# Batch 0's q and k in quarters, masks of the first four pairs added by TensorE, batch 1's loads from another queue: one change at the start of a fused attention and MLP kernel

## The chip, the cores and the metric

The kernel runs on one core of a Trainium2 chip. Its time is the device time in microseconds (us) of one execution; several executions are taken and their median is given. One more execution is recorded by the hardware profiler, and every duration below is from that one. The engines are named as in the profile: PE (matrix multiplications, with PEld for its weight loads), DVE (vector), ACT (activations), POOL (GpSimd), SP (it only issues transfers here).

## What is computed

Sliding-window attention (each position sees 32 positions to either side) over 8 batches, 8 heads, 576 positions of 64 values, followed by an MLP with an ELU-like activation over all 4608 tokens:

```
mask = |i - j| <= 32
x    = softmax(where(mask, q k^T / 8, -1e9)) v          # heads side by side: 4608 x 512
h    = x @ w_in                                         # 512 -> 2048
out  = where(h > 0, h, exp(min(h, 0)) - 1) @ w_out      # 2048 -> 512
```

Inputs and output are f32; inside, the kernel multiplies in bf16.

## The kernel before, in words

**Attention.** A block is 64 queries of one batch, with the 128 keys around them; 9 blocks a batch, 72 in all. Two blocks make a pair (128 tokens), numbered 0 to 35; pair 4 holds the last block of batch 0 and the first of batch 1. The steps of the start, by their names in the plan:

- **L** (`load_qk`, L214): half of the heads of q or k of a batch, one DMA of 576 KB, into a staging tile `stg` of 96 partitions by 4 heads by 6 positions of 64 values (so 1536 contiguous bytes a piece in memory); there are four such buffers. For batch 0 q is issued from ACT and k from SP, for all other batches both from ACT.
- **C** (`cast`, L222): f32 to bf16 in SBUF. Batch 0: q on DVE, k on ACT (L232, L230). Later batches: POOL (L232).
- **T** (L234): six transposes by PE (96 x 128 each) of two heads, into PSUM. For batch 0 four PSUM buffers are used in turn (`psT` and three of `psH`), later one.
- **E** (L246): the copy from PSUM to `qT` or `kT`, by ACT, or by DVE for k of batch 0 (L255, L257). T and E come eight times a batch.
- **QK** (L288): 16 or 24 small matmuls for the scores of a pair, into `psS`, of which there is one buffer, so QK(i+1) waits for SM(i). It needs all eight E of its batch.
- **SM** (L307): exp over the pair, 128 x 1024, by ACT, into `pu`. No maximum is subtracted.
- **MK** (L312): two multiplications on DVE by 0/1 masks, from `pu` into `pm`.
- **AV** (L324): two groups of eight matmuls with v, which has a column of ones for the softmax's sum; **RN** (L342) divides by it on DVE; **X/XE** (L352, L364, L370) transposes the result by PE and copies it by ACT (by DMA from pair 8 on).

v comes straight as bf16 by POOL's DMAs (**LV**, L265), and DVE copies parts of it into the other half of the partitions for odd blocks of batches 0 and 1 (**SV**, L282, L284). The weights come by POOL's DMAs too (**WI** L466, **WO** L471), in an order with LV that is written out by hand (`RING`, L488). DMAs of POOL wait for the eighth one before them.

**MLP.** Pairs are gathered in tiles (2, 2, then 4 eight times). **H** (L381) makes 128 of the 2048 columns for a tile: 4 matmuls, in three PSUM buffers. EX (exp, ACT, L389), FF (ACT L399 or DVE L401) and GG (DVE, L407 or L410) make the activation; **Y** (L424) multiplies by w_out, and the result is copied out and stored from SP.

**The order.** Each engine works its instructions strictly in the order in which the program has them. That order comes from `Plan` (L21): a list scheduler on the host, run once when the program is built. Each step has an engine, an assumed duration, a rank and steps that it depends on, and in the model the plan takes the ready step of the least rank. Dependences and durations in the plan only make the order; on the chip an instruction waits for data and for buffers to come free, not for the plan. For example (L507) the loads of batch 1 stand behind SM(2):

```
                if b == 1:
                    deps.append(("SM", L1AT))
                if b == 2:
                    deps.append(("LV", 1, 8))
                if b:
                    deps.append(("C", b - 1, nm, half))
                P.op(("L", b, nm, half), "ACT" if b or nm == "q" else "SP", 0.45,
```

Ahead of the plan, POOL builds the masks (L682 to L706) and DVE clears borders (L708 to L715).

Of the kernel before, what the change touches and what calls it, by code (L numbers as in the profile page):

```python
# [8 lines left out]
FP32 = mybir.dt.float32  # L9
BF16 = mybir.dt.bfloat16  # L10
AX = mybir.ActivationFunctionType
# [139 lines left out]
def kernel(  # L151
# [17 lines left out]
    QB = 64  # L169
    NQB = S // QB  # L170
    HP = H // 2
    PR = 96
    TPP = S // PR
    KW = S + 2 * WIN
    NPAIR = N_TOK // 128
    NFO = D_FF // 128
# [19 lines left out]

    ident = const.tile([128, 128], BF16)
    masks = const.tile([128, 4, QB], BF16)
    w_in_sb = const.tile([128, NDO, D_FF], BF16)
    w_out_sb = const.tile([128, NFO, DM], BF16)  # L200
    NKB = 2
# [9 lines left out]
            for b in range(B) for nm in "qk" for hp in range(HP)}  # L211


    def load_qk(b, nm, half, eng):  # L214
        src = {"q": q, "k": k}[nm]
        t = stg.tile([PR, HP, TPP * D], FP32, name="stg", tag="stg")
        eng.dma_start(
            out=t, in_=src[b, half * HP:(half + 1) * HP].rearrange(
                "h (p t) d -> p h (t d)", t=TPP))
        live[nm, b, half] = t  # L220

    def cast(b, nm, half, eng):  # L222
        if (nm, b) not in live:
            live[nm, b] = bfp.tile([PR, TPP, H, D], BF16, name="bf", tag="bf")
        t = live[nm, b]
        src = live.pop((nm, b, half)).rearrange("p h (t d) -> p h t d", t=TPP)
        dst = t[:, :, half * HP:(half + 1) * HP, :].rearrange(
            "p t h d -> p h t d")
        if eng is nc.scalar:
            nc.scalar.copy(dst, src)  # L230
        else:
            eng.tensor_copy(dst, src)  # L232

    def T(b, nm, hp):  # L234
        src = live[nm, b]
        n = 2 * hp + (nm == "k")
        if b == 0 and n % 4:
            pt = psH_p.tile([128, TPP, PR], BF16, name="psH", tag="psH")
        else:
            pt = psT_p.tile([128, TPP, PR], BF16, name="psT", tag="psT")  # L240
        for j in range(TPP):
            nc.tensor.transpose(pt[:, j, :], src[:, j, 2 * hp:2 * hp + 2, :],  # L242
                                ident[0:PR, 0:PR])
        live["T", b, nm, hp] = pt

    def E(b, nm, hp):  # L246
        pt = live.pop(("T", b, nm, hp))
        if nm == "k":
            dst = kT[b % NKB][:, hp, WIN:WIN + S]
        else:  # L250
            dst = qT[b % NKB][:, hp, :]
        dst = dst.rearrange("c (p t) -> c p t", t=TPP)
        src = pt.rearrange("c t p -> c p t")
        if EVAC[b, nm, hp] == "ACT":
            nc.scalar.copy(dst, src)  # L255
        else:
            nc.vector.tensor_copy(dst, src)  # L257
# [9 lines left out]
    def swapped(b, qb):  # L267
        return b < 2 and qb % 2 == 1
# [16 lines left out]
                            vt[QB:128, w0 - 1:w1 - 1:2])  # L285


    def QK(i):  # L288
        psS = psS_p.tile([128, 2, 2, HP, QB], FP32, name="psS", tag="psS")
        for s in range(2):  # L290
            b, qb = divmod(2 * i + s, NQB)
            for h in range(H):
                hp, base = h // 2, 64 * (h % 2)
                rhs = qT[b % NKB][base:base + 64, hp, qb * QB:qb * QB + QB]
                lo = qb * QB
                if swapped(b, qb):
                    parts = ((0, QB, lo + QB), (QB, 128, lo))
                else:
                    parts = ((0, 128, lo),)
                for p0, p1, c in parts:  # L300
                    nc.tensor.matmul(  # L301
                        psS[p0:p1, h % 2, s, hp, :],
                        lhsT=kT[b % NKB][base:base + 64, hp, c:c + p1 - p0],
                        rhs=rhs, start=True, stop=True)
        live["S", i] = psS

    def SM(i):  # L307
        pu = pup.tile([128, 2, 2, HP, QB], BF16, name="pu", tag="pu")
        nc.scalar.activation(pu, live.pop(("S", i)), AX.Exp, scale=SCALE)  # L309
        live["U", i] = pu  # L310

    def MK(i):  # L312
        pu = live.pop(("U", i))
        p = pm[i % NPB]
        for s in range(2):
            b, qb = divmod(2 * i + s, NQB)
            m = masks[:, 1 if qb == 0 else 2 if qb == NQB - 1 else
                      3 if swapped(b, qb) else 0, :]
            mb = _bap(m, [m.ap[0], [0, 2], [0, HP], m.ap[1]])
            dst = p[:, :, s * 2 * QB:s * 2 * QB + QB].rearrange(  # L320
                "p (a two) c -> p two a c", two=2)
            nc.vector.tensor_mul(dst, pu[:, :, s], mb)  # L322
# [131 lines left out]
        p0 += n  # L454
    NT = len(tiles)
    NC0 = 4
    NPX = 8

    P = Plan({"SP": 0.8, "ACT": 0.8, "POOL": 5.2, "DVE": 6.0})
# [18 lines left out]
    def prank(i):  # L478
        return PER * tiles[where[i][0]][0] + PER * (i - tiles[where[i][0]][0]) - LEAD - 16

    casts0 = {("q", 0): "DVE", ("k", 0): "ACT", ("q", 1): "DVE",
              ("k", 1): "ACT"}
    engs = {"DVE": nc.vector, "ACT": nc.scalar, "POOL": nc.gpsimd}
    cdur = {"DVE": 1.05, "ACT": 1.5, "POOL": 1.5}
    SVOF = {}


    RING = ([("LV", 0, 0), ("LV", 0, 2), ("LV", 0, 4), ("WI", 0),  # L488
# [10 lines left out]
    for b in range(B):  # L499
# [1 line left out]
        r0 = need - 60  # L501
        t0 = where[b * NQB // 2][0]
        early = [("H", max(t0 - 2, 0), 2 if b == 2 else 8)] if b > 1 else []
        for half in range(2):
            for nm in ("q", "k"):
                deps = list(early)
                if b == 1:  # L507
                    deps.append(("SM", L1AT))
                if b == 2:
                    deps.append(("LV", 1, 8))  # L510
                if b:
                    deps.append(("C", b - 1, nm, half))
                P.op(("L", b, nm, half), "ACT" if b or nm == "q" else "SP", 0.45,
                     r0 + half, deps,
                     lambda b=b, nm=nm, half=half: load_qk(
                         b, nm, half,
                         nc.scalar if b or nm == "q" else nc.sync),
                     dma=1.85, wt=0.085, solo=0.75)
                eng = casts0[nm, half] if b == 0 else "POOL"
                deps = [("L", b, nm, half)]  # L520
                if b >= 2:
                    deps += [("T", b - 2, nm, hp) for hp in range(HP)]
                P.op(("C", b, nm, half), eng, cdur[eng], need - 30 + half, deps,
                     lambda b=b, nm=nm, half=half, eng=eng:
                     cast(b, nm, half, engs[eng]))
        deps = list(early)
        if b > 1:
            deps += [("WO", c) for c in range(NWC)]
        if b == 0:
            deps.append(("C", 0, "q", 0))  # L530
        if b >= NVB:
            last = ((b - NVB + 1) * NQB - 1) // 2
            deps += [("AV", last, 0), ("AV", last, 1)]
# [22 lines left out]
        for hp in range(HP):  # L556
            for nm in ("q", "k"):
                n = hp * 2 + (nm == "k")
                deps = [("C", b, nm, hp // 2)]
                m = n - (4 if b == 0 else 1)  # L560
                if m >= 0:
                    deps.append(("E", b, "qk"[m % 2], m // 2))
                elif b:
                    deps.append(("E", b - 1, "k", HP - 1))
                P.op(("T", b, nm, hp), "PE", 0.3, need - 36 + 4 * n, deps,
                     lambda b=b, nm=nm, hp=hp: T(b, nm, hp))
                deps = [("T", b, nm, hp)]
                if b >= NKB:
                    last = ((b - NKB + 1) * NQB - 1) // 2
                    deps.append(("QK", last))  # L570
                P.op(("E", b, nm, hp), EVAC[b, nm, hp], 0.7, need - 36 + 4 * n, deps,
                     lambda b=b, nm=nm, hp=hp: E(b, nm, hp))

    for c in range(NWC):
        P.op(("WI", c), "POOL", 0.85, RING.index(("WI", c)) - 999, [],
             lambda c=c: WI(c), dma=2.55, wt=0.1, soft=ring(("WI", c)))
        P.op(("WO", c), "POOL", 0.85, RING.index(("WO", c)) - 999,
             [("C", 0, "k", 1)] if c == 0 else [],
             lambda c=c: WO(c), dma=2.55, wt=0.1, soft=ring(("WO", c)))

    for i in range(NPAIR):
# [3 lines left out]
                for hp in range(HP)]  # L585
        if i:
            deps.append(("SM", i - 1))
        P.op(("QK", i), "PE", 0.5, r, deps, lambda i=i: QK(i))
        deps = [("QK", i)]
        if i >= 2:  # L590
            deps.append(("MK", i - 2))
        P.op(("SM", i), "ACT", 1.05, r, deps, lambda i=i: SM(i))
        deps = [("SM", i)]
        if i >= 2:
            deps += [("AV", i - 2, 0), ("AV", i - 2, 1)]
        P.op(("MK", i), "DVE", 1.0, r, deps, lambda i=i: MK(i))
        t, c = where[i]
        for g in range(2):
            deps = [("MK", i)]
            for x in (2 * i, 2 * i + 1):  # L600
                b, qb = divmod(x, NQB)
                if qb % 2 == 0:
# [76 lines left out]
    with tc.manual_schedule():  # L679
# [11 lines left out]
        for lo, key in ((0, QB), (QB, 0)):  # L691
# [12 lines left out]
            fill=0.0, base=(128 - WIN) - 1, pattern=[[0, QB]],  # L704
            channel_multiplier=-1)
        nc.gpsimd.tensor_copy(masks, mf)  # L706
        for t in vw:
            nc.vector.memset(t[0:WIN, 0, :, 0:D], 0.0)  # L708
            nc.vector.memset(t[128 - WIN:128, NQB - 1, :, 0:D], 0.0)
            nc.vector.memset(t[:, 0:NQB:2, :, D:VW], 1.0)  # L710
# [36 lines left out]
```

## Time and profile before

| | us |
|---|---|
| median of 11 runs | 343.91 (342.13 to 346.87) |
| the profiled execution | 343.12 |
| its span, first to last instruction | 341.4 |
| PE busy / DVE / ACT / POOL | 309.8 / 233.8 / 207.3 / 85.4 |
| first transpose begins, QK(0) ends | 9.68, 18.66 |
| SM(0) ends, AV(0) begins | 19.73, 20.47 |
| first H matmul begins | 27.36 |
| batch 1's loads issued, its last cast ends | 22.54 to 24.98, 43.37 |
| first scores with data of batch 1 (pair 4) | 50.67 |

The profiled execution is 0.8 us shorter than the median, which lies within the spread of the runs. In lines of the profile a name such as `psH<-xt,w_in_sb` gives the tile written and those read, `x8` the number of instructions merged into the line, and what stands in square brackets is how long the engine was idle before and what ended that. "Busy" for PE comes from modelled ends of pipelined matmuls, so a busy PE is not one at its peak.

### The profile page before, as it was taken

Reading aid. Unit: us, or ns where it says so; the run is one execution under the profiler, and the core shown is the slowest. Engines: PE = TensorE matmul, PEld = TensorE weight load, DVE = VectorE, ACT = ScalarE, POOL = GpSimd, SP = SyncE. Lnnn points to the kernel's source line nnn. Section 1 sums busy time; section 2 is a strip of 40 time slices with the busy share of each in tenths; the row PEclk is TensorE's granted clock in tenths of the full one; section 3 lists DMA queues with packets and bytes.
Section 4 is the critical chain, followed back from the end, with each engine's and each line's share of the span. In section 5 each row is a group of like instructions: output and inputs, shape, how many; then the busy total and the mean of one; then the engine's idle time right before and its main releaser. Section 6 shows DMA issues by size and latency. Waiting matters only on the chain.

```text
span 341.4 us, 7194 instructions
## 1 busy us (share of the span) xinstructions
PE 309.8 (91%) x2803; PEld 169.4 (50%) x2848; DVE 233.8 (68%) x522; ACT 207.3 (61%) x355; POOL 85.4 (25%) x96
## 2 busy tenths in 40 slices
PE   0468789989889999999999999999999999999995
PEld 0457566554454555545555555455544544444442
DVE  4587678946886788759766976698677767655500
ACT  2546887768777567655865586657655565444511
POOL 8632650650361047006500740050000000000000
PEclk9999999999999999999999999999999999999999
DMA  7999999797989499949955894683211121200021
GB/s 186 191 198 265 236 148 188 189 147 64 239 111 156 111 217 122 162 98 260 129 115 121 242 125 108 134 222 95 79 47 48 46 48 46 79 32 31 33 92 62
DMA packets 78385, 44.55 MB, mean 130 GB/s; under 512 B 54160, under 2 KB 73872, under 8 KB 78352
## 3 DMA queue, kind: packets, MB, share of 16 engines
q0 software_dynamic: 41728, 8.92, 38.5%
q1 hardware_dynamic: 24480, 17.36, 22.3%
q10 hardware_dynamic: 12144, 17.83, 21.4%
q8 instruction: 22, 0.36, 0.5%
q14 instruction: 11, 0.09, 0.1%
HBM read 36.70 MB, written 9.44 MB: 135 GB/s over the span
## 4 chain that ended last, share of the span: by engine, by line
PE 80%; DMA 7%; DVE 7%; ACT 3%; issue 2%; POOL 0%; ACTq 0%
PE psH L381 32%; PE psY L424 32%; DMA stg<-in_q_dram 7%; PE psO L334 5%; PE psT L242 4%; PE psS L301 3%; DVE f L401 2%; DVE pm L322 1%; DVE g L410 1%; PE psO L424 1%; PE psS L424 1%; PE psT L424 1%; DVE g L407 1%; ACT e L389 1%; DVE xs L349 1%
## 5 line engine op out<-in xcount | busy, mean ns | idle before, releaser
L381 PE MATMUL psH<-xt,w_in_sb 128*128 128x512 bf16 (+1 forms) x623 | 146.9, 359 | 4.6 <-DVE g L410 2.1
L389 ACT ACTIVATE e<-psH 128x512 f32<-128x512 f32 (+1 forms) x160 | 88.0, 554 | 83.6 <-PE psH L381 80.9
L424 PE MATMUL psY<-w_out_sb,g 128*128 128x512 bf16 x500 | 128.9, 379 | 2.4 <-issue 1.4
L381 PEld LDWEIGHTS <-w_in_sb 128*128 128x128 bf16 x640 | 59.5, 98 | 57.7 <-issue 5.5
L424 PEld LDWEIGHTS <-g 128*128 128x128 bf16 x576 | 52.2, 98 | 54.7 <-issue 0.6
L232 POOL CAST bf<-stg 96x1536 bf16<-96x1536 f32 x28 | 41.6, 1484 | 136.8 <-DMA stg<-in_k_dram 109.5
L401 DVE TENSOR_SCALAR f<-e 128x512 bf16<-128x512 f32 (+1 forms) x108 | 54.8, 508 | 27.9 <-ACT e L389 27.6
L410 DVE TENSOR_TENSOR g<-psH,f 128x512 bf16<-128x512 f32 (+1 forms) x108 | 70.2, 650 | 3.2
L407 DVE SCALAR_TENSOR_TENSOR g<-f,psH 128x512 bf16<-128x512 bf16 (+1 forms) x52 | 31.3, 601 | 25.3 <-ACT f L399 25.2
L309 ACT ACTIVATE pu<-psS 128x1024 bf16<-128x1024 f32 x36 | 36.8, 1023 | 7.0 <-PE psS L301 3.9
L242 PE MATMUL psT<-ident,bf 96*128 96x96 bf16 x348 | 24.9, 208 | 15.7 <-DVE bf L232 13.0
L242 PEld LDWEIGHTS <-bf 96*128 96x128 bf16 x384 | 23.6, 103 | 25.2 <-DVE bf L232 13.2
L265 POOL DMA_DIRECT2D vw<-in_v_dram x40 | 34.5, 875 | 4.6 <-DMA w_in_sb<-in_moe_w_in_dram 1.8
L334 PEld LDWEIGHTS <-pm 128*128 128x128 bf16 x576 | 27.0, 101 | 14.3 <-DVE pm L322 2.7
L322 DVE TENSOR_TENSOR pm<-pu,masks 128x512 bf16<-128x512 bf16 x72 | 32.9, 498 | 0.8 <-ACT pu L309 0.5
L334 PE MATMUL psO<-vw,pm 128*128 128x65 bf16 x544 | 29.7, 196 | 1.7 <-DVE pm L322 0.7
L349 DVE TENSOR_TENSOR xs<-psO,rc 128x256 bf16<-128x256 f32 x68 | 28.9, 424 | 2.4
L399 ACT ACTIVATE f<-e 128x512 bf16<-128x512 f32 (+1 forms) x52 | 29.5, 567 | 1.3
L347 DVE RECIPROCAL rc<-psO 128x4 f32<-128x4 f32 x68 | 12.2, 180 | 22.7 <-PE psO L334 22.1
L255 ACT COPY qT<-psT 128x576 bf16<-128x576 bf16 x30 | 19.0, 634 | 8.1 <-PE psT L242 8.0
L434 ACT COPY y<-psY 128x512 f32<-128x512 f32 x33 | 18.9, 574 | 5.0 <-remote 4.3
L255 ACT COPY kT<-psT 128x576 bf16<-128x576 bf16 x28 | 17.8, 637 | 5.2 <-PE psT L242 5.1
(45 smaller groups left out, 91.1 us busy)
## 6 DMA issues: line engine op xcount, KB each, us to landing
stg<-in_q_dram ACTq DMA_DIRECT2D x16, 576.0 KB, 10.8
out_dram<-y SPq DMA_DIRECT2D x35, 256.0 KB, 2.5
stg<-in_k_dram ACTq DMA_DIRECT2D x14, 576.0 KB, 8.5
vw<-vw SPq DMA_DIRECT2D x12, 260.0 KB, 5.0
vw<-in_v_dram POOLq DMA_DIRECT2D x24, 128.0 KB, 7.9
w_in_sb<-in_moe_w_in_dram POOLq DMA_DIRECT2D x4, 512.0 KB, 13.0
w_out_sb<-in_moe_w_out_dram POOLq DMA_DIRECT2D x4, 512.0 KB, 23.7
vw<-in_v_dram POOLq DMA_DIRECT2D x16, 96.0 KB, 8.1
```

What stands on the lines that cost most here:

```text
L232: eng.tensor_copy(dst, src)
L242: nc.tensor.transpose(pt[:, j, :], src[:, j, 2 * hp:2 * hp + 2, :], ident[0:PR, 0:PR])
L255: nc.scalar.copy(dst, src)
L309: nc.scalar.activation(pu, live.pop(("S", i)), AX.Exp, scale=SCALE)
L322: nc.vector.tensor_mul(dst, pu[:, :, s], mb)
L334: nc.tensor.matmul(o[:, j, :], lhsT=p[:, h, s * QB:s * QB + 128], rhs=vw[b % NVB][:, qb, h, :], start=(s == 0), stop=(s == 1))
L381: nc.tensor.matmul(ps, lhsT=w_in_sb[:, do, fo * 128:(fo + 1) * 128], rhs=xts[t][:, do, :], start=(do == 0), stop=(do == NDO - 1))
L389: nc.scalar.activation(e, ps, AX.Exp)
L401: nc.vector.tensor_scalar(f, e, -1.0, 0.0, ALU.add, ALU.min)
L407: nc.vector.scalar_tensor_tensor(gs[t][:, fo, :], f, -1.0, ps, ALU.mult, ALU.max)
L410: nc.vector.tensor_tensor(gs[t][:, fo, :], ps, f, ALU.max)
L424: nc.tensor.matmul(ps, lhsT=gs[t][:, fo, c * 128:(c + 1) * 128], rhs=w_out_sb[:, fo, :], start=(fo == 0), stop=(fo == NFO - 1))
```

## The change

- Batches 0 and 1 are staged in 128 partitions: 64 partitions for each of two heads, 9 positions a partition, so 2304 contiguous bytes a piece. Batch 0's q and k come in four loads of two heads each, two loads to a staging buffer; batch 1's still in two. Casts follow the loads, so batch 0 has eight casts (q on DVE, k on ACT), and T of a pair of heads depends only on the cast of its own quarter.
- T of batches 0 and 1 becomes 18 transposes of 64 x 64, in alternating halves of the array, instead of six.
- For pairs 0 to 3, MK is gone. A second tile, `bias`, holds 0 where the mask is 1 and -1e30 where it is 0. PE adds it to the scores with an identity matmul: two of 512 columns ahead of QK (`BM`, which opens the accumulation) and the same two behind it (which close it). SM becomes two activations of 128 x 512 that write `pm` directly.
- In the plan, SM of these pairs stands behind AV of two pairs before; batch 0's V loads stand behind the cast of the third q quarter instead of the first q half; assumed durations follow.
- Batch 1's q and k loads are issued from SP instead of ACT; later batches stay on ACT. In the plan they still stand behind SM(2).

The core of the diff:

```
+    TPW = S // QB
+    NWB = 2
+    bias = const.tile([128, 4, QB], BF16)
...
+    def wide(b):
+        return b < NWB
+    def NH(b):
+        return 4 if b == 0 else 2
     def load_qk(b, nm, half, eng):
...
+        n = NH(b)
+        src = src[b, half * H // n:(half + 1) * H // n]
+        if wide(b):
+            if half % (n // 2) == 0:
+                live["L", nm, b] = stg.tile([128, HP // 2, TPW * D], FP32,
+                                            name="stg", tag="stg")
+            t = live["L", nm, b]
+            if n > 2:
+                t = t[:, half % 2:half % 2 + 1]
+            src = src.rearrange("(n a) (p t) d -> (a p) n (t d)", a=2, t=TPW)
...
     def T(b, nm, hp):
...
+        if wide(b):
+            for j in range(TPW):
+                for a in (0, QB):
+                    nc.tensor.transpose(pt[a:a + QB, j, :],
+                                        src[a:a + QB, hp, j, :],
+                                        ident[a:a + QB, a:a + QB])
+            return
...
+    def biased(i):
+        return i < NBM
+    def add_mask(i, psS, par, last=False):
+        k0, k1 = (kind(*divmod(2 * i + s, NQB)) for s in range(2))
+        m = bias[:, k0, :]
+        nc.tensor.matmul(
+            psS[:, par], lhsT=ident,
+            rhs=_bap(m, [m.ap[0], [(k1 - k0) * QB, 2], [0, HP], m.ap[1]]),
+            start=not last, stop=last)
+    def BM(i):
+        psS = psS_p.tile([128, 2, 2, HP, QB], FP32, name="psS", tag="psS")
+        live["S", i] = psS
+        add_mask(i, psS, 0)
+        add_mask(i, psS, 1)
...
-                        rhs=rhs, start=True, stop=True)
+                        rhs=rhs, start=first,
+                        stop=first)
         live["S", i] = psS
+        if biased(i):
+            add_mask(i, psS, 0, True)
+            add_mask(i, psS, 1, True)
     def SM(i):
+        if biased(i):
+            psS = live.pop(("S", i))
+            for par in range(2):
+                dst = pm[i % NPB][:, par::2, :].rearrange(
+                    "p a (s c) -> p s a c", c=QB)
+                nc.scalar.activation(dst[:, 0::2], psS[:, par], AX.Exp,
+                                     scale=SCALE)
+            return
...
+    NBM = 4
+    V0AT = 2
-                P.op(("L", b, nm, half), "ACT" if b or nm == "q" else "SP", 0.45,
+                P.op(("L", b, nm, half), "ACT" if b > 1 or (b == 0 and nm == "q")
+                     else "SP", 0.45,
...
-            deps.append(("C", 0, "q", 0))
+            deps.append(("C", 0, "q", V0AT))
...
+        if biased(i):
+            P.op(("BM", i), "PE", 0.45, r - 4, deps[-1:] if i else [],
+                 lambda i=i: BM(i))
+            deps.append(("BM", i))
...
+            deps += ([("AV", i - 2, 0), ("AV", i - 2, 1)] if biased(i)
+                     else [] if biased(i - 2) else [("MK", i - 2)])
...
+        nc.gpsimd.tensor_scalar(bias, mf, -1.0, 1e30, ALU.add, ALU.mult)
```

## The prediction, made before the changed kernel was run

> **What bounds the kernel now.** I read the table of windows first, since the share over the whole span (PE 91%) hides the stages. Columns: start:end, length, then busy us of PE, its weight loads, DVE, ACT, POOL, then clock, DMA share and GB/s.
>
> ```profile
> 14.00:19.78 5.78, 2.98 (x49) 2.58 (x50) 4.20 (x8) 3.52 (x4) 3.36 (x5) 1.00 1.70 189
> 19.78:27.36 7.58, 6.41 (x128) 5.33 (x128) 6.32 (x20) 4.14 (x5) 2.04 (x3) 1.00 1.33 213
> 27.36:30.00 2.64, 2.64 (x19) 2.01 (x19) 1.51 (x7) 1.09 (x3) 0.00 (x0) 1.00 1.16 268
> 30.00:44.00 14.00, 10.44 (x102) 7.69 (x102) 10.68 (x26) 10.88 (x29) 8.92 (x8) 1.00 1.30 241
> 44.00:320.00 276.00, 267.76 (x2405) 142.21 (x2448) 201.89 (x442) 179.06 (x303) 59.91 (x54) 1.00 0.80 122
> ```
>
> From 44 us on PE is the bound: 8.2 us idle in 276. PE's idle time that a change of the start can reach lies before 44: about 9.7 us before the first transpose, most of 10 to 19.78, then 1.2 us in 19.78 to 27.36 and 3.6 us in 30 to 44. So a gain must bring PE to its dense stage earlier, and PE work that is added counts unless it falls into one of those holes. Next the chain of waits in order of time, for the head:
>
> ```profile
> 1.26 12.81 DMA stg<-in_q_dram
> 14.09 0.97 DVE bf L232
> 15.10 0.66 PE psT L242 x6
> 15.76 1.45 PE psH L242 x18
> 17.24 0.77 DVE kT L257
> 18.06 0.62 PE psS L301 x15
> 18.70 1.03 ACT pu L309
> ...
> 22.89 12.23 DMA stg<-in_q_dram
> 35.17 1.47 POOL bf L232
> ```
>
> Two transfers are in it: batch 0's last half of q (landed at 14.07) and a load of batch 1 (issued at 22.89, landed at 35.12). Last the timeline, for the state of PE and of ACT's queue. The number after the engine's start is the time of the merged group, "x" its instructions:
>
> ```profile
> 19.78 0.76 PE L301 MATMUL psS<-qT,kT 64*128 64x64 bf16 x24 [1.12 <-ACT pu L309]
> 22.89 0.51 ACTq L217 DMA_DIRECT2D stg<-in_q_dram  x1
> 27.36 1.87 PE L381 MATMUL psH<-xt,w_in_sb 128*128 128x256 bf16 x8 [0.23 <-ACT xt L370]
> 36.69 0.43 PE L242 MATMUL psT<-ident,bf 96*128 96x96 bf16 x6 [1.08 <-POOL bf L232]
> 53.28 0.54 PE L301 MATMUL psS<-qT,kT 64*64 64x64 bf16 x24
> ```
>
> The same 24 score matmuls take 0.76 us at 19.78 and 0.54 us at 53.28. Eight AV matmuls (L334) go from 0.62 to 0.41, and four H matmuls from 0.85 (at 29.48) to 0.60 (30.73). PE runs slow until about 30 us, though the page's clock row shows no throttle.
>
> **What the Trainium skill says.** "TensorE: Matmul & The Clock Gate", Part 1: an idle array runs at half clock and goes to full clock after one window of some 3.4 us of sustained matmuls; a 512-column matmul costs 426.7 ns cold, 215.7 warm. The trace agrees: warm ones are 0.86 us for four (chain of waits, L424); cold, 1.87/8 x 2 gives at most 0.47 for 512 columns. Scores and AV, with PE busy 6.41 of 7.58 us, did not warm it in 19.78 to 27.36; 2.5 us of H did. The same page, Part 4, says transposes don't count as activity. "DMA: Bandwidth & Descriptors", section "Issuing engines are not separate DMA queues": which engine issues a DMA changes only the time at the issuer. The trace shows that time on ACT: four issues between 22.54 and 24.98, and the third SM, whose scores are ready at 24.35, begins at 25.50. "SBUF — State Buffer", "Who interferes with whom": a GpSimd operation and a DVE one in a two-port mode exclude each other. Trace: L401 at 41.96 takes 1.55 us instead of 0.29, beside a POOL cast from 41.91.
>
> **The change, part by part.** All times are in the profiled execution (span 341.4, its own time 343.1, 1.7 around it); the median shown, 343.9, is 0.8 higher, so I carry the difference over to it.
>
> A. Quarters and 64-partition staging, batch 0. The bytes stay; one contiguous run grows from 1536 to 2304 B. The queue table gives ACT's queue 24480 packets of 709 B in 22.3% of 16 x 341.4 us, 50 ns each; if half of that is cost per packet, a third fewer packets save a sixth of the 12.8 us, 2.1, and if none of it is, 0; below nothing only if batch 1's loads, now behind k on SP, share the engines with the last q. I take 0.5: 13.6. From landing to the end of QK(0) it was 18.66 - 14.07 = 4.6 us. Now: ACT's cast of 576 elements a partition, 0.67 ("ScalarE: Activation LUTs", "What ACT_TABLE_LOAD costs": 186 ns + 0.833 per element; the trace's 1472 ns for 1536 is just that), or DVE's 0.956 x 576/1536 = 0.36; one transposing step of 18 small transposes, 0.65 (24 matmuls of such size take 0.76 cold); E 0.77; the 18 last matmuls of QK(0), 0.6; handovers 0.15. Sum 2.85, saving 1.75. QK(0) ends at 13.6 + 2.85 = 16.4 instead of 18.66: **2.25 earlier**. The other six steps run under the later quarters' transfer; without that cover the six T would cost about 4 us.
>
> B. Masks by PE. Each of pairs 0 to 3 gets two 512-column matmuls before QK and two after: 16, or 6.9 us cold and 3.5 warm. The first two come before QK(0) and hide in its wait for data. The two after it cost 0.86, and SM in two halves is 2 x 0.61 = 1.22 instead of 1.02 (same rule for 512 elements). SM(0) ends at 16.4 + 0.86 + 0.04 + 1.22 = 18.5, against 19.73: **1.2 earlier** is left. MK (0.76 a pair on DVE) goes, so AV(0) starts at about 18.5 instead of 20.47. But behind SM(0) PE has little room: the 6.4 us of QK(1..3), AV(0..2) and two XT up to 27.36, and now 12 bias matmuls, 5.2 cold: 11.6 us of cold work. Does it warm PE? Nearly unbroken work with 45% of dense 512-column matmuls should, one or two windows after 18.5; I take 23. By then 3.9 us of it are done (0.6 of waits on SM); the other 7.7 cost 0.6 of their cold time (0.66 for AV, 0.71 QK, 0.5 bias) = 4.6, with 0.3 of waits: H could start at 27.9, **0.5 later** than 27.36. The H matmuls that ran cold until 30 (1.87 + 0.85 for 12) then take 12 x 0.13 = 1.6, with one AV group 0.2 less: **1.4 back**. Net at 30 us: 0.9 ahead. Bounds: warm at 20.5, 2.5 us ahead; cold until H, see the second rival. On POOL, the bias tile costs one more operation of 128x256, 0.4 us as the cast to masks (L706, 396 ns), ahead of all V and W issues (first at 5.18); the first V lands at 14.9 and is used by PE from 18.5, so nothing.
>
> C. Batch 1's loads on SP. SP has nothing else until its first output at 53, so they go out as soon as a staging buffer is free (about 8 to 14 us) and not at 22.5; the plan's dependence on SM(2) only orders them. Behind them on SP is nothing. ACT loses four issues (2.4 us; already used above, as SM(3) no longer waits). The loads should land by about 28 instead of 41.9, and POOL's casts follow its W and V issues, from about 27. That ends the wait of 1.08 us at 36.69; of the other 2.5 us of PE idle in 30 to 44 (H chains of ACT and DVE, 0.87 behind the slowed L401) I take 0.4: **1.5 gained**, bounds 0 and 3. Cost: V and W now share with 2.36 MB of f32. w_in's first chunk was in by 18.6 by POOL's next issue, 9 us before H; V for pair 0 landed from 14.9. I take 0, bounds 0 and 2.
>
> D. Batch 1 transposed in 64 pieces: 8 steps of 18 at 20 ns (0.47 for 24 in the chain) to 25 instead of 0.26: 0.8 to 1.5 in all, **0.9 lost**, in a stage where PE fills; below nothing excluded, since the columns streamed double. POOL's casts for it shrink to 3/4 (1152 elements). The order of all later steps shifts too: 0, plus or minus 1 (the 8.2 us idle after 44).
>
> Sum: -0.9 - 1.5 + 0.9 = **-1.5 us**: 341.6 for this execution, **342.4** against the median.
>
> **Rivals.** *The dense start opens up* (0.27): PE warms at once and batch 1's early data fills the hole of 30 to 44. For: that hole is 3.6 us, POOL waited 11.3 us for those loads before 45. Against: ACT and DVE are each busy over 10.6 of these 14 us, so the H chains stay. -2.5 - 3.0 + 0.9 = -4.6: 339.3. *Masks on a cold PE* (0.27), slower: the array isn't warm until H. 11.6 + 0.9 of waits from 18.5 is 31.0, 3.6 later than 27.36; H warm gives 1.4 back, C 1.0, D costs 0.9: +2.1, 346.0. For: PE stayed cold through 85% busy time before; against: the dense matmuls are what warmed it then. It decides for the worse from a warm-up later than about 26. *The loads starve V* (0.06): on SP they run before V, AV(0) waits past 18.5 for it and the gain of A is gone: about 344.5. Forecast as above: 0.40.
>
> **How the numbers follow.** A measurement of this kernel (342.1 to 346.9 in 11 runs) tells some 0.5%, 1.7 us, from no change: faster is below 342.2, slower above 345.6. The forecast's own range is 341 to 344, about four tenths of it faster. Faster: 0.27 + 0.16 = 0.43. Slower: most of the cold rival, a little of the starved one, 0.25. Same: 0.32. Low is the first rival with some room, 339.0, high the cold one with half a microsecond, 346.6.
>
> **What would show it.** A: a last QK(0) matmul near 16.4. B: 512-column matmuls of 0.43 in pair 0 and 0.22 by pair 2; H near 28 with 0.13 a matmul from its first. C: batch 1's casts ending near 32 on POOL, no wait of T on them. D: 18 transposes in over 0.36. Wrong if AV(0) waits for V, or if PE's hole in 30 to 44 stays at 3.6 us.

## The result and the profile after

The changed kernel takes 350.2 us, the median of 12 runs (346.16 to 353.87), against 344.2 for the kernel before beside it. Ratios, here and below, leave out the executions that are over 1.5% slower than the fastest of the same kernel (4 of these 12), while medians and ranges count all. The ratio is 1.0136, with an interval of 1.0100 to 1.0173: **slower by 1.4%**, some 4.7 us; the two medians lie 6.0 us apart. The forecast was 342.4, with a range of 339.0 to 346.6. The profiled execution has a span of 348.7 us, against 341.4.

The table of windows of the kernel after, with the columns of the prediction's first fence:

```profile
14.00:19.78 5.78, 4.37 (x49) 2.24 (x48) 2.58 (x8) 1.29 (x3) 1.49 (x2) 1.00 1.25 283
19.78:27.36 7.58, 6.60 (x76) 3.45 (x74) 3.20 (x11) 2.93 (x6) 3.35 (x5) 1.00 1.45 203
27.36:30.00 2.64, 2.64 (x40) 1.83 (x35) 1.14 (x1) 1.05 (x3) 2.42 (x3) 1.00 1.24 206
30.00:44.00 14.00, 9.83 (x107) 6.75 (x105) 11.04 (x24) 8.80 (x24) 8.78 (x10) 0.88 1.65 190
44.00:320.00 276.00, 264.09 (x2470) 140.73 (x2512) 201.75 (x438) 178.94 (x305) 56.49 (x49) 1.00 0.69 119
```

Three things are to be seen. In 19.78 to 27.36 PE is as busy as before (6.60 us against 6.41) but gets 76 matmuls done, not 128; six of the 76 are masks of 512 columns, which take 3.1 of the 6.60 us. In 30 to 44, where step C was to fill a hole of 3.6 us, the hole is 4.2 us, and here the clock column falls below 1 (0.88), as it does nowhere in the kernel before's table. After 44 PE idles 11.9 us instead of 8.2.

The chain of waits in order of time, for the head of the kernel after:

```profile
6.77 8.92 DMA vw<-in_v_dram
16.05 0.54 PE psO L409 x7
...
19.58 1.09 ACT pm L381 x2
...
24.28 1.09 ACT pm L381 x2
...
31.86 1.45 DVE f L476
...
34.08 1.67 DVE f L476
35.77 0.44 DVE g L485
36.25 2.73 PE psH L456 x12
```

Before, the chain began with batch 0's last half of q and went through QK(0). Now it begins with **v of batch 0**, then goes from one pair's SM to the next, 4.7 us apart, and then through two DVE instructions of line 476 that are given 1.45 and 1.67 us. That line is L401 in the kernel before (line numbers are those of each run's own kernel), and is 0.29 us when nothing disturbs it.

The timeline of the kernel after, for what surrounds these links:

```profile
6.86 0.39 SPq L239 DMA_DIRECT2D stg<-in_k_dram  x1
...
12.84 0.59 PE L365 MATMUL psS<-qT,kT 64*128 64x64 bf16 x18 [0.59 <-DVE kT L295]
13.37 1.04 PE L337 MATMUL psS<-bias,ident 128*128 128x512 bf16 x2
...
16.05 0.54 PE L409 MATMUL psO<-vw,pm 128*128 128x65 bf16 x7 [0.73 <-DVE vw L320]
...
27.18 1.17 POOL L256 CAST bf<-stg 128x1152 bf16<-128x1152 f32 x1
...
28.68 0.61 PE L456 MATMUL psH<-xt,w_in_sb 128*128 128x256 bf16 x4
...
31.77 1.52 DVE L476 TENSOR_SCALAR f<-e 128x256 bf16<-128x256 f32 x1
31.98 1.16 POOL L256 CAST bf<-stg 128x1152 bf16<-128x1152 f32 x1
...
33.81 1.03 PE L456 MATMUL psH<-xt,w_in_sb 128*128 128x256 bf16 x8 [1.61 <-DVE g L485]
34.00 1.74 DVE L476 TENSOR_SCALAR f<-e 128x256 bf16<-128x256 f32 x1
34.43 1.16 POOL L256 CAST bf<-stg 128x1152 bf16<-128x1152 f32 x1
...
36.25 3.72 PE L456 MATMUL psH<-xt,w_in_sb 128*128 128x256 bf16 x20 [1.41 <-DVE g L485]
```

Read it from below. The 20 H matmuls at 36.25 take 3.72 us, 0.19 each; warm ones take 0.13. PE has gone back to half speed after two waits of 1.61 and 1.41 us for DVE's g. The table of windows says the same, 0.69 as the mean of 34 to 38 us and 0.50 within 36 to 38:

```profile
30.00:34.00 4.00, 1.63 (x26) 1.18 (x24) 3.23 (x8) 2.35 (x7) 2.99 (x4) 1.00 1.25 210
34.00:38.00 4.00, 2.59 (x17) 1.81 (x16) 3.12 (x6) 1.74 (x5) 2.83 (x4) 0.69 1.54 189
```

DVE was late because two instructions of line 476 ran beside two POOL casts of batch 1 and took 1.52 and 1.74 us (run 10 tests this). The cast at 27.18 has no bracket: it waited for no transfer. Its load went out from SP at 6.86 and had long landed; the cast stood in POOL's queue behind v and weight issues, which wait for earlier transfers (the one at 25.55 had waited 1.69 us for a piece of w_in). So batch 1's data came early, and nobody could use it early. T(1), which uses it, comes at 39.9 in PE's fixed order.

The way from one stage to the next, from the traces (us from the span's start; H0, H1 and so on are the H matmuls of the first, second and later tiles). The other columns are kernels of the next section:

| | before | after | act_loads | thin_cast | q_gated |
|---|---|---|---|---|---|
| first weight load of H0 | 26.9 | 28.3 | 24.6 | 27.0 | 22.0 |
| last of H0 | 42.4 | 45.1 | 38.9 | 40.7 | 36.0 |
| last of H1 | 63.0 | 68.3 | 61.1 | 62.3 | 57.2 |
| last of H2 | 97.6 | 105.1 | 96.1 | 97.6 | 95.3 |
| last of H3 | 129.3 | 136.9 | 128.6 | 130.0 | 128.6 |

All of the loss is there by H2: 7.5 us, of which 1.4 before H0, 1.3 in it, 2.6 up to the end of H1 and 2.2 up to the end of H2. Against act_loads, which has the same order of work, the kernel after is 9.0 us behind by then: 3.7 before H0, 2.5 in it, 2.8 up to the end of H2.

### The profile page after: what moved, and what is told of

It reads as the page before. It is cut to its first block, busy times and chain, and to the rows that moved or that the text cites. A ratio compares the mean times of both kernels' runs of the same rounds, so it can differ in the third digit from the quotient of the medians.

```text
span 348.7 us, 7618 instructions
## 1 busy us (share of the span) xinstructions
PE 319.1 (92%) x3010; PEld 171.0 (49%) x3056; DVE 236.2 (68%) x516; ACT 207.0 (59%) x361; POOL 84.4 (24%) x97
## 4 chain that ended last, share of the span: by engine, by line
PE 82%; DVE 8%; ACT 3%; DMA 3%; issue 2%; POOL 1%; ACTq 0%; POOLq 0%
PE psH L456 34%; PE psY L499 31%; PE psO L409 5%; PE psS L365 3%; PE psT L281 3%; DVE f L476 3%; DMA vw<-in_v_dram 3%; PE psS L337 2%; DVE pm L397 1%; DVE g L485 1%; PE psO L499 1%; PE psS L499 1%; PE psT L499 1%; DVE xs L424 1%; DVE g L482 1%
## 5 line engine op out<-in xcount | busy, mean ns | idle before, releaser
L476 DVE TENSOR_SCALAR f<-e 128x512 bf16<-128x512 f32 (+1 forms) x108 | 56.0, 519 | 28.5 <-ACT e L464 28.3
L264 POOL CAST bf<-stg 96x1536 bf16<-96x1536 f32 x24 | 35.6, 1484 | 137.0 <-DMA stg<-in_k_dram 127.7
L303 POOL DMA_DIRECT2D vw<-in_v_dram x40 | 34.0, 865 | 11.4 <-DVE rc L422 4.7
L385 ACT ACTIVATE pu<-psS 128x1024 bf16<-128x1024 f32 x32 | 32.7, 1023 | 4.2 <-PE psS L365 4.0
L409 PEld LDWEIGHTS <-pm 128*128 128x128 bf16 x576 | 26.2, 100 | 17.6 <-ACT pm L381 4.3
L281 PEld LDWEIGHTS <-bf 96*128 96x128 bf16 x288 | 17.2, 98 | 11.3 <-issue 2.0
L281 PE MATMUL psT<-ident,bf 96*128 96x96 bf16 x288 | 20.2, 206 | 1.8 <-ACT kT L293 0.8
```

Source lines behind the costliest of these rows:

```text
L303: nc.gpsimd.dma_start(out=vt[r:r + hi - lo, qb, :, 0:D], in_=vb[lo:hi])
L409: nc.tensor.matmul(o[:, j, :], lhsT=p[:, h, s * QB:s * QB + 128], rhs=vw[b % NVB][:, qb, h, :], start=(s == 0), stop=(s == 1))
L476: nc.vector.tensor_scalar(f, e, -1.0, 0.0, ALU.add, ALU.min)
```

## Experiments

Three theories stood at first, with the numbers used in the first four expectations. **1, masks**: the 512-column mask matmuls run at half speed and delay every pair. **2, casts**: batch 1's early data lets POOL's casts collide with DVE. **3, order**: the plan puts later steps in a worse order. That the loads, free to go out at 7 us, take DMA time from v and the weights was added as a theory before run 5. Ratios are against the kernel before, with their intervals.

**1. nobias: no masks on PE.** `NBM` also enters the plan, so the order of the work changes with it.

```
-    NBM = 4
+    NBM = 0
```

> All of the change, but masks of all pairs by DVE as before (no mask matmuls; the plan is made anew). Theory 1 (the mask matmuls run on a cold PE inside the chain of pairs): the pair period falls from 4.7 to about 2 us, H begins near 21 to 23 instead of 28.7, and the time falls by 5 to 8 us, to 342 to 345. Theory 2 (batch 1's early casts collide with DVE and PE goes cold again): the hole of 31 to 37 us stays, the time falls by 0 to 2 us. Theory 3 (the plan's new order of later steps costs it): the order changes anew, no definite number, H(2) to H(9) as far apart as before would speak against it.

Measured: 348.37 us, ratio 1.0129 (1.0079 to 1.0179). Without any mask on PE, in an order of its own, the kernel is as slow as with them.

**2. thin: the order of the kernel after, masks of 64 columns instead of 512.**

```
-            psS[:, par], lhsT=ident,
-            rhs=_bap(m, [m.ap[0], [(k1 - k0) * QB, 2], [0, HP], m.ap[1]]),
+            psS[:, par, 0, 0, :], lhsT=ident, rhs=m,
```

> All of the change in the same order, but each of the 16 mask matmuls has 64 columns instead of 512, so that most scores of pairs 0 to 3 stay unmasked. Only PE time of the mask matmuls goes. Theory 1: 16 x (0.43 - 0.05) = 6 us at the start, of which the end gets 4 to 6: 344 to 346. Theory 2: at most 1 us, since the casts of batch 1 still collide. Theory 3: no change, 349 to 351, since the order of all steps is the same.

Measured: 348.11 us, ratio 1.0164 (1.0129 to 1.0199). H0 begins at 25.4 instead of 28.3, but its first 12 matmuls then run at half speed (eight in 1.91 us), the two collisions of line 476 stay (1.79 and 1.74 us), and H0 ends at 44.0. The masks theory fails as the explanation of the loss.

**3. before_bias: the kernel before with only the masks of pairs 0 to 3 moved to PE** (the `BM`, `QK` and `SM` parts of the diff, with their plan).

```
+    NBM = 4
+        nc.gpsimd.tensor_scalar(bias, mf, -1.0, 1e30, ALU.add, ALU.mult)
```

> The kernel before with only the masks of pairs 0 to 3 by PE added. Theory 1: slower than before by 5 to 9 us (pair period 4.7 us instead of 1.9, three periods, less 1 us for the late first mask step): 349 to 353. Theory 2: as before within 2 us, since batch 1's loads and casts come as late as before. Theory 3: undecided.

Measured: 351.28 us, ratio 1.0231 (1.0182 to 1.0281). By itself, in an order of its own, the mask part costs a good deal: H0 begins at 31.7. So it is not innocent everywhere; what it costs in the kernel after is priced by runs 2 and 11, which keep that kernel's order.

**4. act_loads: the kernel after, its order on every engine kept, but batch 1's loads issued from ACT behind SM(2), as before.**

```
-                         nc.scalar if b > 1 or (b == 0 and nm == "q")
+                         nc.scalar if b or nm == "q"
                           else nc.sync),
```

> All of the change in the same planned order, but batch 1's loads are issued from ACT at the same place of the order (behind SM(2)), not from SP. Theory 1: within 2 us of the changed kernel, ACT's issues lie beside the mask matmuls: 349 to 352. Theory 2: the casts of batch 1 come later and off the H chain's start, 346 to 348.

Measured: 343.73 us, ratio 1.0004 (0.9978 to 1.0030). One condition on the issuing engine takes the whole loss away, more than either theory had expected. Its timeline:

```profile
12.58 0.61 PE L337 MATMUL psS<-bias,ident 128*128 128x512 bf16 x2
...
13.88 0.29 PE L409 MATMUL psO<-vw,pm 128*128 128x65 bf16 x2 [0.69 <-ACT pm L381]
...
21.96 0.39 ACTq L239 DMA_DIRECT2D stg<-in_k_dram  x1
...
24.82 0.60 PE L456 MATMUL psH<-xt,w_in_sb 128*128 128x256 bf16 x4
...
29.10 1.14 POOL L256 CAST bf<-stg 128x1152 bf16<-128x1152 f32 x1 [7.53 <-DMA stg<-in_k_dram]
30.59 0.58 DVE L476 TENSOR_SCALAR f<-e 128x256 bf16<-128x256 f32 x1
...
33.51 0.81 DVE L476 TENSOR_SCALAR f<-e 128x256 bf16<-128x256 f32 x1
```

AV(0) waits for ACT and no longer for v, and starts at 13.88; in the kernel after one of its matmuls starts at 15.09 and the others only when v is there, at 16.05. The loads go out 15 us later (21.96), and yet the first cast starts only 1.9 us later than in the kernel after, because there POOL was not free for it. The four casts now wait for their data one by one, from 29.1 to 37.6, and line 476 still takes 0.58, 0.81 and, at 35.70, 1.04 us beside them.

**5. quarters_only: no masks on PE and batch 1's loads from ACT in the plan too**, so in an order of its own.

```
+    NBM = 0
+                P.op(("L", b, nm, half), "ACT" if b or nm == "q" else "SP", 0.45,
```

> Quarters and 64-partition staging alone: batch 1's loads from ACT behind SM(2), masks of all pairs by DVE. Theory A (two losses: the early loads cost some 6 us by taking DMA time from v and the weights, the mask matmuls cost some 5 us on a cold PE, and the quarters gain what both lose): 5 us below the changed kernel with loads on ACT, 337 to 340. Theory B (the early loads are the only loss; masks by PE are free, and the quarters gain nothing at the end): 342 to 345.

Measured: 348.16 us, ratio 1.0144 (1.0100 to 1.0187): as slow as the kernel after, though it has neither masks on PE nor early loads, and outside both ranges. H0 begins at 21.9 and H1 ends at 56.7, 6.3 us ahead of the kernel before; then H2 begins at 77.3, 4.8 us behind it. Between them PE waits 4.62 us, until 63.38, for a POOL cast of batch 2 on which the transposes (L281) depend, and then runs at half speed: the granted clock is 0.50 from 62 to 68 us. So here the lead ran into data of batch 2 that weren't there yet. What the order of this plan adds isn't separated, and runs with orders of their own (1, 3, 5, 7, 8, 12) are compared with the kernel after with care; 1, 7 and 12 share one order.

**6. gated: the kernel after with the loads still on SP, but held there.** SP first issues a copy of 128 B that reads the output of SM(2).

```
+        if b == 1 and half == 0 and nm == "k":
+            nc.sync.dma_start(out=gate, in_=live["G"])
         eng.dma_start(out=t, in_=src)
...
+            if i == L1AT:
+                live["G"] = pm[i % NPB][0:1, 1, 0:QB]
```

> All of the change, with batch 1's loads issued from SP, but SP first issues a copy of 128 B that reads what SM(2) wrote, so that they start when SM(2) is done and not before. If it is the early start that costs: as with the loads on ACT or up to 1 us better, 341.5 to 344.5. If it is the queue (SP beside ACT): as the changed kernel, 348 to 351.

Measured: 346.41 us, ratio 1.0053 (1.0022 to 1.0083), 0.8% below the kernel after in the same order, and between the two ranges. The profile shows the copy issued at 22.95, the loads going out at 23.68 and H0 beginning at 24.6. So with the loads on SP all the same, holding them takes most of the loss away: most of it lies in the time of the loads and not in the queue. The remaining 0.5% above act_loads isn't explained; the two intervals just overlap.

**7. q_gated: the same gate without masks on PE**, in the order of run 1.

```
-    NBM = 4
+    NBM = 0
+            nc.sync.dma_start(out=gate, in_=live["G"])
...
+        if i == L1AT:
+            live["G"] = pu[0:1, 1, 0, 0, :]
```

> No mask matmuls, quarters, batch 1's loads from SP behind SM(2) by the same copy of 128 B. Theory A: 336 to 340, the best of all, as ACT is spared 2 us of issues. Theory B: 342 to 345.

Measured: 343.68 us, ratio 0.9934 (0.9900 to 0.9967): the lowest ratio of all. But the median of all its 22 runs lies only 0.1% below the 343.89 us of the kernel before beside it, so **a gain over the kernel before isn't shown**. Against run 1, with the same plan, the gate alone is worth 2% (1.0129 against 0.9934), or 1.7% by the medians of all runs.

**8. before_sp: the kernel before with only the issuing engine of batch 1's loads changed**, in the plan and in the code.

```
-                P.op(("L", b, nm, half), "ACT" if b or nm == "q" else "SP", 0.45,
+                P.op(("L", b, nm, half), "ACT" if b > 1 or (b == 0 and nm == "q") else "SP", 0.45,
...
-                         nc.scalar if b or nm == "q" else nc.sync),
+                         nc.scalar if b > 1 or (b == 0 and nm == "q") else nc.sync),
```

> The kernel before with batch 1's loads issued from SP, with nothing that holds them back. If the early start costs by itself: 346 to 350, with the first AV waiting for v. If it costs only together with the quarters (which need v earlier): 342 to 345.

Measured: 359.99 us, ratio 1.0457 (1.0384 to 1.0531), from 4 runs, far above both ranges. The timeline of this kernel:

```profile
9.44 0.31 SPq L217 DMA_DIRECT2D stg<-in_k_dram  x1
...
28.20 0.29 DVE L282 COPY vw<-vw 64x520 bf16<-64x520 bf16 x1 [6.09 <-DMA vw<-in_v_dram]
29.31 0.90 PE L334 MATMUL psO<-vw,pm 128*128 128x65 bf16 x8 [5.29 <-DVE pm L322]
...
32.66 1.87 PE L381 MATMUL psH<-xt,w_in_sb 128*128 128x256 bf16 x8 [0.23 <-ACT xt L370]
```

Here the starving of v is seen whole: DVE stands 6.09 us for a v tile, MK (L322) behind it on DVE, and AV behind that. It isn't the first AV, which starts at 20.15 as before, but a later one. In the records of the packets, the queue of v and the weights moved 594 packets between 18 and 22 us; in the kernel before it was 1680.

**9. small_loads: the order of the kernel after, the loads early, but only 64 of 1152 values a partition are loaded**; the casts spread these, so they are as long as before. The attention of batch 1 is computed from them.

```
+        if b == 1:
+            eng.dma_start(out=t[:, 0, 0:D], in_=src[:, 0, 0:D])
...
+                src = _bap(m, [m.ap[0], [0, n], [0, TPW], m.ap[1]])
```

> The changed kernel in the same order, but batch 1's four early loads bring only 64 of 1152 values a partition (half the pieces, 256 B each), and its casts spread these; all other work is the same, the casts can run as early as before. If the loss is the DMA time taken from v and the weights: as the kernel with held loads or a little better, 341 to 345, with AV(0) near 14 us. If it is the early casts' collision with DVE: unchanged or worse, 348 to 352.

Measured: 345.29 us, ratio 1.0028 (1.0002 to 1.0053). With the traffic gone, nearly the whole loss is gone. Its profiled execution (span 347.5) is the slowest of its 20 runs, so I take only the order of events from it: AV(0) starts at 14.96 without a wait for v, and the casts run from 22.1 to 30.6, so that three of the four are over before H needs DVE. Line 476 (here L483) is undisturbed:

```profile
27.04 1.16 POOL L263 CAST bf<-stg 128x1152 bf16<-128x1152 f32 x1
...
29.45 1.16 POOL L263 CAST bf<-stg 128x1152 bf16<-128x1152 f32 x1
...
31.16 0.28 DVE L483 TENSOR_SCALAR f<-e 128x256 bf16<-128x256 f32 x1
```

The mask matmuls of pair 3 still run at half speed at 27.2.

**10. thin_cast: full early loads, but POOL casts only 64 of the 576 values of each pair of heads**, and T(1) reads these nine times, so batch 1's attention is computed from them.

```
+                if b == 1:
+                    dst, src = dst[:, :, 0:D], src[:, :, 0:D]
...
-                                        src[a:a + QB, hp, j, :],
+                                        src[a:a + QB, hp, 0 if b == 1 else j, :],
```

> The changed kernel in the same order with its full early loads, but POOL casts only 64 of 576 values of each head pair of batch 1 (and the transposes use these nine times). If the collision of POOL's casts with DVE at 31 to 37 us costs: 344 to 347. If the DMA time is all of it: 348 to 351.

Measured: 344.95 us, ratio 1.0022 (0.9996 to 1.0047). Taking the length of the casts away while the traffic stays recovers as much as run 9. Row 30 to 44 of its table of windows:

```profile
30.00:44.00 14.00, 12.37 (x158) 8.37 (x161) 10.44 (x28) 10.93 (x30) 6.58 (x9) 1.00 1.72 188
```

Against the row of the kernel after, PE does 158 matmuls instead of 107 and its clock stays at 1. H0 still begins late (27.0), AV(0) still waits for v until 15.97, but H0 takes 13.7 us instead of 16.8. The four casts start at nearly the same times as in the kernel after (27.35, 29.55, 32.05 and 34.49, against 27.18, 29.45, 31.98 and 34.43), so it is their length beside DVE's work, 0.3 to 0.4 us instead of 1.16, that makes the difference.

**11. thin_gated: gated with the thin masks of run 2.**

> The kernel with batch 1's loads on SP held until SM(2), and the 16 mask matmuls of 64 columns instead of 512 (most scores of pairs 0 to 3 unmasked), same order. With early loads the thin masks changed nothing. If PE time of the masks counts once the loads are held: 3 to 5 us below the held kernel with full masks, 339 to 343. If it never counts: 344 to 347.

Measured: 343.80 us, ratio 1.0002 (0.9972 to 1.0032), against 1.0053 for gated: once the loads are held, the columns of the masks cost at most about 0.5%; the two intervals overlap.

**12. q_gate1: q_gated, held only until SM(1).**

```
-            if i == L1AT:
+            if i == 1:
```

> No mask matmuls, quarters, batch 1's loads on SP held by the copy of 128 B, but only until SM(1) instead of SM(2), some 2 us earlier. If each us of early load costs by taking DMA time from v and w: between the kernel held at SM(2) and the one not held (0.993 and 1.013 of before), nearer to the former: 0.995 to 1.0. If only loads beside batch 0's own q and k cost: 0.99 to 0.995, as held at SM(2).

Measured: 343.68 us, ratio 0.9977 (0.9949 to 1.0005). It lies in the range of the first theory, but the interval overlaps that of q_gated, so the two aren't told apart: holding the loads for one pair less brings no gain.

## Why the prediction was wrong

**Step A, quarters: right in kind, too small.** QK(0) ended at 13.4, not 16.4; 5.3 us earlier, not 2.25. The cast of the last q began at 10.30, where it had been 14.09; the steps behind it took 3.1 us, near the 2.85 of my sum. So the mis-sized term is the landing. I worked from a packet's time that I took to be at least half in proportion to its bytes, and from the wrong row: q1, which I called ACT's queue, is SP's, and ACT's is q10. The packet records of the first 6 us say (mean bytes and time of a packet):

```
          q1 (SP)            q10 (ACT)
before    1507 B  97 ns      1531 B  93 ns
after     2089 B  106 ns     2068 B  94 ns
```

So in these 6 us a packet of 2.1 KB took nearly as long as one of 1.5 KB, and the page's first slice moves 274 GB/s instead of 186. The layout in SBUF changed along with the packets (128 partitions instead of 96), and no run separates the two. My upper bound of 2.1 us for the landing should have been near 4.

**Step B, masks on PE: near on H, by luck.** I put H at 27.9; its first matmul began at 28.68. But the head started 3 us earlier than I took, and PE warmed up at about 28.7 instead of 23: two 512-column masks take 1.04 us up to 27.2 and still 1.00 at 27.85, and the four H matmuls at 28.68 take 0.61, which is full speed. The two errors nearly cancel. Rival two, "masks on a cold PE", describes this head well, and the time it gave, 346.0, lies nearer than the forecast. Yet it isn't the cause: the thin masks of run 2 left the kernel at 1.0164, with the loads held they bring at most about 0.5% (run 11), and act_loads keeps the full masks and loses nothing. The V tiles, at "nothing", did cost: with the early loads beside them, AV(0) waited for v.

**Step C, batch 1's loads on SP: this step failed.** I wrote "1.5 gained" and for the sharing with v and the weights "I take 0, bounds 0 and 2". Measured with the order held, it loses: 1.0136 against 1.0004 (act_loads) and 1.0053 (gated), and 1.0129 against 0.9934 in the order without masks; 0.8 to 2%, 3 to 7 us. Without C my sum is 0 (0.9 gained by A and B, 0.9 lost by D), and act_loads, which leaves C out, measures 1.0004. That agreement is luck in part: there the first H matmul begins at 24.82, 2.5 us earlier than before and not 0.5 later, and the lead is down to 0.7 us by the end of H3. Three parts of the reasoning of step C failed.

- *The gain.* I read the 11.3 us that POOL waited for these loads as time to be won. But PE's order puts T(1) between the H matmuls. The loads went out 15 us earlier than in act_loads, POOL's first cast came 1.9 us earlier, and PE's hole in 30 to 44 grew from 3.6 to 4.2 us.
- *The traffic.* "DMA: Bandwidth & Descriptors", section "Issuing engines are not separate DMA queues", in the Trainium skill says that transfers of all engines interleave on the same 16 DMA engines. The trace agrees: between 14 and 18 us the queue of v and the weights moved 850 packets, in act_loads 1581, and AV(0) waits for v, which the prediction had named as the sign of being wrong. Rival three, at 0.06, had this mechanism; its 344.5 counted only the lost gain of A. But the wait of AV(0) alone isn't the loss: thin_cast, with 743 packets in those 4 us and the same wait, is at 1.0022.
- *The time of the casts.* I let the casts follow POOL's issues "from about 27" and called it a gain, though H was to begin at 27.9. They then fall one behind another on the first H's, 27.2 to 35.6. "SBUF — State Buffer", "Who interferes with whom", in the Trainium skill, which I had cited for just this collision, agrees with the trace: beside the casts the instructions of line 476 took 1.52 and 1.74 us, and with shorter casts (run 10) at most 0.86. PE waited 1.61 and 1.41 us and went back to half speed. I had priced one such collision in the kernel before and didn't ask what an earlier cast would hit.

Traffic and casts aren't two shares of a sum: taking either away leaves 1.0028 or 1.0022. The traffic holds back v and the weights, and with them POOL's queue, so that the casts come due together just as H begins (the first at 27.2); without the traffic most of them come before it (the first at 22.1), and without their length they don't hurt there. The same collision comes back with batch 2: at 61.6 one instruction of line 476 takes 1.55 us beside a cast, and PE waits 1.63 us until 63.78. In act_loads one takes 1.44 us at 58.90, but PE's longest wait nearby is 0.63 us. So the collision costs PE more in one order of events than in another. This may be part of the loss between 45 and 105; the rest of it is in small waits that I didn't trace one by one.

**Step D, T(1) in 64-partition pieces: right.** In the chains of waits a step of 18 transposes takes 0.40 us, where the six of before took 0.26; the first line is from the kernel before, the second from the kernel after:

```profile
44.63 0.26 PE psT L242 x6
42.32 0.40 PE psT L276 x18
```

That is 0.14 us for each of 8 steps, 1.1 us in all, where I had put 0.9, with bounds of 0.8 and 1.5. The timeline gives 0.47 and 0.42 us, but there a group ends with the modelled end of its last matmul, while the next matmul starts earlier: 0.40 and 0.26 us after the first transpose. No run changed this part alone.

**Rival one**, the dense start, is seen best with the loads held and no masks: q_gated begins H0 at 22.0, 4.9 us ahead, and leaves 0.5 us of hole in its row of 30 to 44:

```profile
30.00:44.00 14.00, 13.47 (x200) 9.13 (x201) 10.10 (x28) 12.06 (x31) 7.96 (x9) 1.00 1.51 220
```

Even so, little or nothing of it is left at the end. It is 5.8 us ahead at the end of H1, 2.3 at that of H2 and 0.7 at that of H3. PE's waits in 57.2 to 128.6 of this kernel (us in total, times, longest) name the first of the causes, the casts of batch 2:

```profile
PE psT L284 <- POOL bf L267: 2.7, 2, 2.1
PE psT L446 <- ACT kT L296: 1.7, 2, 1.0
```

In the kernel before that wait for POOL doesn't occur in these tiles. Batch 2's loads went out 5.7 us earlier than there (48.24 against 53.93), but the first cast, which waited for its load to land, began only 2.3 us earlier (58.20 against 60.46). So here most of the lead won at the head was given back at the next batch, as in quarters_only. I hadn't asked what is late next.

**What stays open.** How much of the loss of runs 1, 3, 5 and 8 is their own order isn't separated; runs 2, 4, 6, 9, 10 and 11 keep that of the kernel after, and the verdict on step C rests on them. And whether the early loads also keep PE cold longer isn't settled: the masks were at full speed from about 20 us in act_loads and gated, from 25.8 in thin_cast (in these three also for a moment at 12.6), and in the kernel after at no time, as PE warmed up behind the last of them, but also not by 27.2 in small_loads, which has almost no early traffic. With one profile of each, chance in the moment when the clock changes can't be told from the cause.

## What to carry to other kernels

A dependence that exists only in the host's plan doesn't hold a transfer: on an idle queue it started here as soon as its buffer was free, at 6.86 us, though the plan had put it behind SM(2), which began at 24.28; and it shared the DMA engines with what was urgent. Before moving a load forward, look for who can use it early, what lands later because of it, and which engine's work it makes due at a new time; if it must leave the busy engine, hold it with a small copy that reads the result it should wait for. In these runs a lead won at the head was worth only what the next batch's data could keep.

## What was not expected of the hardware

- A packet's time hardly depended on its size between 1.5 and 2.1 KB (97 and 106 ns on SP's queue, 93 and 94 ns on ACT's) in the first 6 us, where the number of partitions changed too.
- The table of "TensorE: Matmul & The Clock Gate", Part 1, in the Trainium skill has the array go back to half clock after an idle window of some 3.4 us; a later paragraph there tells of a kernel whose many short idles also made the clock change. Here it went back without one gap of that length: the longest were 1.61 and 1.41 us, with PE busy 1.63 of the 4 us from 30 to 34, and the granted clock was 0.69 in 34 to 38. In act_loads it went back at 13.6, as the masks of 1.04 us at 15.13 show, after 3.4 us with PE busy for 2.22 and no wait over 0.7. The measurement decides: shorter gaps are enough. How much idle time it takes isn't known from these runs.
- In act_loads, gated and thin_cast the first six score matmuls, at 11.3 to 11.4, take 0.26 us (0.34 in the kernel after), and two masks at 12.6 to 12.7 take 0.61: full speed, though from 6.8 to the first of them PE had run nothing but transposes. The prediction had it from Part 4 of the same page that transposes don't count as activity for the clock; these three traces speak against it, and the measurement decides.
- PE also stayed at half clock from 13.4 to about 28.7 us in the kernel after, though it was busy 6.60 of 7.58 us in 19.78 to 27.36.
- The DVE instructions at 31.77 and 34.00 are recorded as beginning 0.21 and 0.43 us before the POOL casts beside them, and still take 1.52 and 1.74 us: these recorded starts don't tell which of the two has to wait. (Starts on POOL are rough, and the first of the two overlaps the DVE instruction before it, which ends at 31.85.)
